# A scan and a mixture of adapters on one core: expert weights A loaded in whole rows, first units alone, SyncE holding transfers back

## The chip, the cores and the metric

The kernel runs on one core of one Trainium2 chip. The metric is the device time of one execution in microseconds; the time of a kernel is the median of its runs. The engines are called as in the profile: PE (TensorE), PEld (its weight loads), DVE (VectorE), ACT (ScalarE), POOL (GpSimd) and SP (SyncE, which here only issues transfers). HBM is the memory that holds inputs and outputs.

## The reference

Two steps are computed, both in float32. First a linear recurrence along the sequence, for 8 batches of 6400 steps and 128 channels:

```python
h = np.zeros((B, D), dtype=np.float32)
for t in range(S):
    h = a[:, t] * h + b[:, t]
    out[:, t] = h
```

Its result, seen as N = 51200 rows x of 128 channels, goes through a mixture of 8 experts of rank 16. For each row the two experts with the highest logits are taken, with softmax weights over the two:

```python
logits = x @ w_gate                                   # N x 8
topk = np.argpartition(-logits, K, axis=1)[:, :K]     # K = 2
...
delta[mask] += w[mask, k, None] * ((x[mask] @ A[e]) @ B[e])
return x + delta
```

A is 8 x 128 x 16 and B is 8 x 16 x 128, 64 KB each.

## The kernel before

The 51200 rows are cut into 100 units of 512 rows. A unit passes these stages (the numbers are the lines of the profile):

- SP loads a and b of two units in one 512 KB transfer each (line 345); a of unit 0, b of units 0 and 1 and a of unit 99 come alone, 256 KB each. Each of a and b has a ring of 8 slots of two units.
- PE transposes both into PSUM against an identity (492), so that channels lie on partitions and time along the row.
- ACT copies a out of PSUM (526, tile a_st).
- DVE runs the recurrence with one scan instruction, and a second where a batch ends in the unit (550). The scans form one serial chain. The result x stays in fp16, transposed, in the tile xT.
- PE multiplies x by the gate and by all of A at once, 8 + 128 = 136 columns per block of 128 rows (589; the 136 columns are cst_h), and ACT copies that to the tile zl (607).
- The gating finds the two best experts and their weights for a group of units: on DVE maxima (662, or 691 and 713), on POOL subtractions (672 to 735), on ACT two relus (656) and a sigmoid (745, tile g). Groups have three units, but the first four and the last ones are smaller; in the first two and the last two groups ("quick") DVE may take over steps of POOL.
- POOL, or DVE near the end, multiplies z by the expert weights (766, tile zw); PE transposes the product (774), DVE or ACT copies it out (782, zwT); PE adds x and the product with B in PSUM (802); ACT copies that to an output buffer (817, outt, 24 units); SP stores two units in one 512 KB transfer, the last two alone.

For most units two neighbours share one layout: 128 partitions hold 8 rows each of 1024. So the product of a unit waits for the scan of both units of its pair (`scanned`, and `x_block` for the layout). The units in `SOLO` have a layout of their own and wait for their own scan. Before the change those are the last two.

The order of all instructions on all engines is made by a planner in the program (`_Plan.schedule`). It goes through operations with assumed costs, latencies and priorities, and writes out one fixed list for each engine. `_Plan.run` then emits each list with semaphore waits on what an operation depends on. An engine works its list in order, so an instruction that waits holds back all that stand behind it. This holds for SP too: its transfers are issued in one fixed order. A load waits until PE has used the slot (`users`, eight pairs back); a store waits for its output copies and for the scan of the unit 20 further on (`HOLD`). Nothing in it waits for another transfer.

At the start POOL makes the identity (351, 358), and ACT issues the loads of the gate weights, B and A, in this order (345). A is read with `moe_A.rearrange("e d r -> d e r")`: 1024 runs of 16 floats, 64 bytes each. POOL casts all three to fp16 (430). PE runs ten matmuls on a zeroed tile (401, "heat") before the first transposes, and two more after each of the first five units (411, "fill"). These compute nothing that is used.

Of the kernel before, what the change touches and what calls it, by code (L numbers as in the profile page):

```python
# [15 lines left out]
    "zr": 48,  # L16
    "nout": 24,
    "hold": 20,
    "heads": (1, 1, 1, 1),
    "group": 3,  # L20
    "tails": (2, 2, 1, 1),
    "quick": (2, 2),
    "split": (4, 4),
    "solo": (0, 2),
    "mul": (0, 1, 0, 8),
    "tev": (1, 1, 4, 4),
    "tail": 8,
    "fills": 5,
    "caps": {'a': 3, 'b': 4, 'Z': 1, 'O': 3, 'w': 8},
    "least": {'Z': 1, 'O': 1},  # L30
    "pairs": (98, 2),
# [32 lines left out]
class _Plan:  # L64


    def __init__(self, sems, latency, weight, offset, switch, banks, caps, least):
# [7 lines left out]
        self.least = least  # L75
        self.ops = {}
# [12 lines left out]
    def schedule(self):  # L89
        ops = self.ops  # L90
        users = {n: [] for n in ops}
        left = {}
        glued = {op.next for op in ops.values() if op.next}
        for op in ops.values():
            op.deps = [ops[d] for d in dict.fromkeys(op.deps) if d in ops]
            left[op.name] = len(op.deps)
            for d in op.deps:
                users[d.name].append(op)
            op.key = self.weight * (op.unit + self.offset.get(op.kind, 0.0))
        end = {}  # L100
# [12 lines left out]
        while todo:  # L113
            best = None
            for e, c in cand.items():
                for x in c:
                    op = x[1]
                    if op.turn is not None and op.turn != turn:
                        continue
                    t = max(free[e], x[0])  # L120
                    takes = op.takes + (ops[op.next].takes if op.next else [])
                    if takes:
                        want = {}
                        for r, _ in takes:
                            want[r] = want.get(r, 0) + 1
                        kept = sum(max(0, k - held[r] - want.get(r, 0)) for r, k in self.least.items())
                        if len(takes) + kept > len(idle) or any(held[r] + k > self.caps[r] for r, k in want.items()):
                            continue
                        t = max(t, idle[len(takes) - 1][0])
                    if op.mode and mode and op.mode != mode:  # L130
                        t += self.switch
                    late = op.busy[e] - min(op.busy.values())
                    if best is None or (t + late, op.key) < best[:2]:
                        best = (t + late, op.key, e, x, t)
            _, _, e, pick, t = best
            for x in pick[1].engs:
                cand[x].remove(pick)
            run = [pick[1]] + ([ops[pick[1].next]] if pick[1].next else [])
            for op in run:
                for role in op.takes:  # L140
                    _, i, giver = idle.pop(0)
                    self.bank_of[role] = i
                    held[role[0]] += 1
                    if giver and giver.eng != e:
                        run[0].deps.append(giver)
            for op in run:
                turn += op.turn is not None
                op.eng = e
                mode = op.mode or mode
                self.order[e].append(op)  # L150
                free[e] = t + op.busy[e]
                t = free[e]
                if op.dma:
                    link = max(link, free[e] + 550.0) + op.dma[2]
                    end[op.name] = link + op.dma[3]
                else:
                    end[op.name] = free[e] + op.lat[e]
                if op.gives:
                    held[op.gives[0]] -= 1
                    idle.append((end[op.name], self.bank_of[op.gives], op))  # L160
                    idle.sort(key=lambda x: x[:2])
                todo -= 1
                for u in users[op.name]:
                    left[u.name] -= 1
                    if not left[u.name] and u.name not in glued:
                        for x in u.engs:
                            cand[x].append((max(end[d.name] for d in u.deps), u))
        self.span = max(end.values())
        for op in ops.values():
            if op.eng == "pe":  # L170
                op.deps = [d for d in op.deps if d.eng != "pe"]
            for d in op.deps:
# [27 lines left out]
def bass_associative_scan_2x2__then__mixture_of_adapters_kernel(  # L200
# [88 lines left out]
    with ExitStack() as stack:  # L289
# [4 lines left out]
        cst_f = sb(nc.sbuf_tensor("cst_f", [128, E + 256], F32))  # L294
        cst_h = sb(nc.sbuf_tensor("cst_h", [128, E + 256], F16))
        warm_t = sb(nc.sbuf_tensor("warm_t", [128, UT], F16))
        warm = sb(nc.sbuf_tensor("warm", [128, 1], F32))
        E_A = E + 128
        wA_h = cst_h[:, 0:E_A]
# [30 lines left out]
        dma_sem = {}  # L330

        latency = {"pe": 205.0, "dve": 170.0, "act": 230.0, "pool": 130.0, "sp": 100.0}
        plan = _Plan(sems, latency, 1000000.0, KEY, 100.0, len(psum), CFG["caps"], CFG["least"])
# [35 lines left out]

        add_dma("wg_in", "act", -110, [(cst_f[:, 0:E], moe_w_gate[:, :])], ("wg",), 80.0, (), "fix", 450.0, 2000.0)  # L370
        add_dma(
            "B_in",
            "act",
            -109,
            [(cst_f[:, E + 128 : E + 256], moe_B.rearrange("e r d -> (e r) d"))],
            ("B",),
            220.0,
            (),
            "fix",
            450.0,  # L380
            3500.0,
        )
        add_dma(
            "A_in",
            "act",
            -108,
            [(cst_f[:, E : E + 128].rearrange("d (e r) -> d e r", e=E), moe_A.rearrange("e d r -> d e r"))],
            ("A",),
            700.0,
            (),  # L390
            "fix",
            450.0,
            5500.0,
        )
        add("w0", "dve", "fix", -109, 60.0, lambda h: h.memset(warm[:, :], 0.0))
        add("table", "act", "fix", -107, 1500.0, lambda h: h.activation(warm[:, :], warm[:, :], ACTF.Sigmoid), ["w0"])
        add("wt", "dve", "fix", -109, 60.0, lambda h: h.memset(warm_t[:, :], 0.0))

        def heat(h):
            for _ in range(10):  # L400
                last = h.matmul(bank(("w", -1))[:, :], warm_t[:, 0:128], warm_t[:, :])
            return last

        add("heat", "pe", "fix", -109, 4000.0, heat, ["wt"], mode="half", takes=[("w", -1)], gives=("w", -1))

        def fill(w):


            def emit(h):
                for _ in range(2):  # L410
                    last = h.matmul(bank(("w", w))[:, :], warm_t[:, 0:128], warm_t[:, :])
                return last

            add(f"fill{w}", "pe", "fix", 1000.0, 440.0, emit, [f"AB{w}"], mode="full", takes=[("w", w)], gives=("w", w))

        for w in range(CFG["fills"]):
# [512 lines left out]
```

## Time and profile before

| | |
|---|---|
| median of 8 runs | 203.12 us (202.79 to 205.71) |
| profiled execution | 203.44 us, of which 201.4 us are the span of the profile |
| mean granted clock of TensorE | 0.992 |
| first scan starts | 6.22 us |
| first maxima of the gating (line 662) start | 12.89 us |
| last scan starts | 183.59 us |
| last output copy (line 817) ends | 198.04 us |
| HBM read, written | 52.56 MB, 26.21 MB; 391 GB/s over the span |
| load or store of 512 KB, issue to landing, median | 15.5 and 15.4 us |
| loads of gate weights, B, A, issue to landing | 3.0, 3.5 and 5.9 us |

All times of a view are counted from the start of the span. The share of an engine is its busy time over the span; instructions that only issue transfers or wait are not counted. Two rows of digits cut the span into 40 slices of some 5 us, and give a share in tenths: the clock that TensorE was granted, and the busy share of the 16 DMA engines (it can come out a little over 1, since packets overlap). The queue q1 is that of SP, q10 that of ACT; q8 brings instructions. The chain of waits is the work that ended last, followed back from the end; an entry there is a start, a duration and what it was. A line in the list of waits is the engine that waited, its line, whom it waited for, and then microseconds in total, times, and the longest.

### The profile page before, as it was taken

The page shows a single profiled execution, that of the slowest core. Times are in us where ns is not written, and L with a number is a line of the kernel's source. Part 1 is how long each engine was busy: PE and PEld are TensorE (multiplying, and loading weights), DVE is VectorE, ACT ScalarE, POOL GpSimd, SP SyncE. Part 2 cuts the span into 40 slices and gives each one's busy share as a digit, 9 for nine tenths or more (in the row PEclk, how much of TensorE's full clock was granted, in tenths as well). Part 3 has the DMA queues.
Part 4 walks back from the last instruction along what each step waited for, and adds up shares of the span by engine and source line. Part 5 has one row for each costly group of instructions (what it writes and reads, how often), then busy time and mean ns, then how long its engine had stood idle before and what let it go on. Part 6 is the DMA issues. An engine that isn't in the chain of part 4 may idle for free.

```text
span 201.4 us, 8187 instructions
## 1 busy us (share of the span) xinstructions
PE 183.6 (91%) x3204; PEld 162.1 (80%) x3204; DVE 171.5 (85%) x296; ACT 179.3 (89%) x461; POOL 157.3 (78%) x280
## 2 busy tenths in 40 slices
PE   7896999999998999997999899989999999999672
PEld 3575888988997988896898789879989889988561
DVE  1497799999999799998879887899799699797980
ACT  2386899999998998998999899999999899999862
POOL 2015378789999797888689799999998999769840
PEclk9997899999999999999999999999999999999999
DMA  6999999999999999999999999999999999986996
GB/s 209 366 410 405 410 405 405 405 409 404 409 414 411 413 418 409 412 413 417 407 411 417 407 412 415 416 413 412 418 410 410 417 410 410 410 340 263 365 408 237
DMA packets 23397, 79.30 MB, mean 394 GB/s; under 512 B 3648, under 2 KB 3776, under 8 KB 23360
## 3 DMA queue, kind: packets, MB, share of 16 engines
q1 hardware_dynamic: 22032, 78.65, 97.6%
q8 instruction: 25, 0.41, 0.8%
q10 hardware_dynamic: 1328, 0.14, 0.5%
q14 instruction: 12, 0.10, 0.1%
HBM read 52.56 MB, written 26.21 MB: 391 GB/s over the span
## 4 chain that ended last, share of the span: by engine, by line
PE 48%; ACT 19%; DVE 11%; issue 7%; DMA 6%; POOL 5%; SPq 2%; DVEq 0%
PE ps L492 17%; PE ps L802 15%; PE ps L589 8%; PE ps L774 7%; ACT zl L607 6%; DVE xT L550 6%; DMA b_in<-in_b_dram 6%; ACT outt L817 5%; ACT a_st L526 4%; POOL zw L766 4%; SPq L345 2%; ACT pn L656 2%; DVE zw L766 2%; DVE zwT L782 2%; ACT g L745 1%
## 5 line engine op out<-in xcount | busy, mean ns | idle before, releaser
L550 DVE TENSOR_TENSOR_SCAN xT<-a_st,xT,ps 128x512 f16<-128x512 f32 x96 | 120.2, 1252 | 14.1 <-ACT a_st L526 8.6
L766 POOL TENSOR_TENSOR zw<-zl,g 128x512 f16<-128x512 f32 x93 | 98.8, 1068 | 7.5 <-ACT g L745 7.5
L607 ACT COPY zl<-ps 128x408 f32<-128x408 f32 (+1 forms) x139 | 71.6, 543 | 0.2
L526 ACT COPY a_st<-ps 128x512 f32<-128x512 f32 x100 | 61.5, 641 | 11.2 <-PE ps L492 10.4
L492 PE MATMUL ps<-ident_f,a_in 64*128 64x64 f32 (+1 forms) x792 | 67.3, 229 | 3.9 <-DMA b_in<-in_b_dram 1.9
L492 PE MATMUL ps<-ident_f,b_in 64*128 64x64 f32 (+1 forms) x792 | 67.6, 230 | 1.9 <-issue 1.5
L492 PEld LDWEIGHTS ps<-ident_f,a_in 64*128 64x128 f32 (+1 forms) x792 | 56.5, 140 | 13.8 <-issue 4.3
L817 ACT COPY outt<-ps 128x512 f32<-128x512 f32 x99 | 60.7, 628 | 3.0 <-PE ps L802 2.4
L492 PEld LDWEIGHTS ps<-ident_f,b_in 64*128 64x128 f32 (+1 forms) x792 | 56.3, 140 | 1.4 <-issue 0.8
L589 PE MATMUL ps<-cst_h,xT 128*128 128x136 f16 x400 | 49.6, 235 | 0.5 <-DVE xT L550 0.2
L802 PE MATMUL ps<-ident_h,xT 128*128 128x128 f16 x400 | 43.1, 230 | 2.3 <-issue 1.3
L774 PE MATMUL ps<-ident_h,zw 128*128 128x128 f16 x400 | 38.7, 220 | 4.0 <-DVE zw L766 2.2
L589 PEld LDWEIGHTS ps<-cst_h,xT 128*128 128x128 f16 x400 | 35.8, 148 | 4.5 <-DVE xT L550 0.7
L802 PE MATMUL ps<-cst_h,zwT 128*128 128x128 f16 x400 | 38.9, 220 | 0.0
L782 DVE COPY zwT<-ps 128x256 f32<-128x256 f32 x89 | 35.8, 409 | 3.5 <-PE ps L774 3.3
L802 PEld LDWEIGHTS ps<-ident_h,xT 128*128 128x128 f16 x400 | 33.4, 148 | 4.7 <-DVE zwT L782 1.9
L774 PEld LDWEIGHTS ps<-ident_h,zw 128*128 128x128 f16 x400 | 25.2, 98 | 7.4 <-DVE zw L766 3.2
L802 PEld LDWEIGHTS ps<-cst_h,zwT 128*128 128x128 f16 x400 | 27.3, 100 | 0.0
L656 ACT ACTIVATE pn<-d 128x96 f32<-128x96 f32 (+2 forms) x72 | 23.1, 331 | 0.1
L735 POOL TENSOR_TENSOR um<-d,pn 128x96 f32<-128x96 f32 (+2 forms) x36 | 14.1, 393 | 7.0 <-ACT pn L656 6.5
L706 POOL TENSOR_TENSOR L<-zl,pn 128x96 f32<-128x96 f32 (+2 forms) x34 | 13.4, 394 | 4.7 <-ACT pn L656 3.7
L728 POOL TENSOR_TENSOR d<-d 128x96 f32<-128x96 f32 (+2 forms) x38 | 13.8, 365 | 1.5 <-DVE d L681 0.6
(31 smaller groups left out, 85.9 us busy)
## 6 DMA issues: line engine op xcount, KB each, us to landing
a_in<-in_a_dram SPq DMA_DIRECT2D x49, 512.0 KB, 15.5
b_in<-in_b_dram SPq DMA_DIRECT2D x49, 512.0 KB, 15.5
out_dram<-outt SPq DMA_DIRECT2D x49, 512.0 KB, 15.4
a_in<-in_a_dram SPq DMA_DIRECT2D x2, 256.0 KB, 9.1
b_in<-in_b_dram SPq DMA_DIRECT2D x2, 256.0 KB, 4.3
out_dram<-outt SPq DMA_DIRECT2D x2, 256.0 KB, 2.8
cst_f<-in_moe_B_dram ACTq DMA_DIRECT2D x1, 64.0 KB, 3.5
cst_f<-in_moe_A_dram ACTq DMA_DIRECT2D x1, 64.0 KB, 5.9
```

The source lines that it names most:

```text
L492: last = h.transpose(*args())
L526: lambda h: h.copy(a_st[w % NAS][:, :], bank(("a", w))[:, :]),
L550: last = h.tensor_tensor_scan(out=x_at(lo, hi), data0=a_st[w % NAS][:, lo:hi], data1=bank(("b", w))[:, lo:hi], initial=init, op0=ALU.mult, ...
L589: last = h.matmul(dst, x_block((b0 + j) // Q, (b0 + j) % Q), wA_h)
L607: return h.copy(zl[:, r0 : r0 + n, :], src)
L656: lambda h: h.activation(v(pn[s]), v(src[s]), ACTF.Relu, bias=bias, scale=scale),
L735: lambda h: h.tensor_tensor(out=v(um[s]), in0=v(d1[s]), in1=v(pn[s]), op=ALU.subtract),
L766: lambda h: h.tensor_tensor(out=oview, in0=zview, in1=gview, op=ALU.mult),
L774: last = h.transpose(dst[:, q * 128 : (q + 1) * 128], zw[v % NZW][:, q, :], ident_h[:, :])
L782: return copy(zwT[v % NZT][:, :].bitcast(F32), bank(("O", v))[:, 0 : UT // 2])
L802: last = h.matmul(bank(("O", v))[:, cols], (x_block(v, q), zwT[v % NZT][:, cols])[part], (ident_h[:, :], Bcat_h)[part], start=part == 0 an ...
L817: return copy(outt[:, v % NOUT, :], bank(("O", v))[:, :])
```

## The change

Five things are changed.

1. A is read as `(e h) (l r)`: partition e*16 + h gets the eight rows l = 0..7 of expert e that belong to block h, 512 bytes in one run, 128 runs in all. The load moves ahead of B's on ACT's queue. To bring this to the layout with d on partitions, DVE and POOL multiply the loaded tile with a mask (`mine`) into `spread`, which holds for each l a 128 x 128 matrix with a partition's values in the columns of its own expert, in fp16; and eight matmuls with 0/1 matrices (`pick`, shifted by one column for each l) add up in one PSUM bank. ACT copies the result to the fp16 tile. `mine`, `high` and `pick` are made on DVE from the identity. POOL's cast of A is gone.
2. Units 0 and 1 join the units that stand alone (`solo`): their products wait for their own scan only, and their store writes rows of 2 KB.
3. The matmuls ahead of the first transposes go from ten to six.
4. Those after the first units go from two after each of five units to two, one and one after the first three.
5. After the planner has fixed all orders, each transfer on SP's list, loads and stores alike, gets a wait for the landing of the transfer four places before it.

The planner's orders come out different on all engines after the first few instructions, since it sees the new operations; the kinds and numbers of the instructions after the start are the same, except for a few steps of the quick groups that go from POOL to DVE and one output copy that goes from DVE to ACT.

```diff
+    "flight": 4,
-    "solo": (0, 2),
+    "solo": (2, 2),
-    "fills": 5,
+    "heat": 6,
+    "filler": (2, 1, 1),
...
         self.span = max(end.values())
+        moves = [op for op in self.order["sp"] if op.dma]
+        for old, new in zip(moves, moves[self.flight :]):
+            new.deps.append(old)
...
+        pick = sb(nc.sbuf_tensor("pick", [128, 8 * 129], F16))
+        high = sb(nc.sbuf_tensor("high", [128, 16], F32))
+        mine = sb(nc.sbuf_tensor("mine", [128, E], F32))
+        spread = sb(nc.sbuf_tensor("spread", [128, 8, E, R], F16))
...
+            "A_in",
+            "act",
+            -109,
+            [(cst_f[:, E : E + 128], moe_A.rearrange("e (h l) r -> (e h) (l r)", l=8))],
...
-            "A_in",
-            "act",
-            -108,
-            [(cst_f[:, E : E + 128].rearrange("d (e r) -> d e r", e=E), moe_A.rearrange("e d r -> d e r"))],
...
-            for _ in range(10):
+            for _ in range(CFG["heat"]):
...
+        add("pick0", "dve", "fix", -109, 330.0, lambda h: h.memset(pick[:, :], 0.0))
+        add("high", "dve", ...
+                out=high[:, :], in_=ident_f[:, :].rearrange("p (e h) -> p h e", e=E), axis=AX.X, op=ALU.max
+        add("pick", "dve", ...
+                pick[:, :].rearrange("p (k c) -> p k c", c=129)[:, :, 0:128:8],
+                high[:, :].unsqueeze(1).broadcast_to([128, 8, 16]),
+        add("mine", "dve", ...
+                out=mine[:, :], in_=ident_f[:, :].rearrange("p (e h) -> p e h", e=E), axis=AX.X, op=ALU.max
+        raw = cst_f[:, E : E + 128].rearrange("p (l r) -> p l r", r=R)
+        for name, eng, lo, hi, time in (("spr0", "pool", 0, 3, 900.0), ("spr1", "dve", 3, 8, 760.0)):
+                lambda h, lo=lo, hi=hi: h.tensor_tensor(
+                    out=spread[:, lo:hi, :, :],
+                    in0=raw[:, lo:hi, :].unsqueeze(2).broadcast_to([128, hi - lo, E, R]),
+                    in1=mine[:, :].unsqueeze(1).unsqueeze(3).broadcast_to([128, hi - lo, E, R]),
+                    op=ALU.mult,
+        def gather(h):
+            for k in range(8):
+                last = h.matmul(
+                    bank(("w", -2))[:, 0:128],
+                    pick[:, k * 128 : (k + 1) * 128],
+                    spread[:, k, :, :].rearrange("p e r -> p (e r)"),
+                    start=k == 0,
+                    stop=k == 7,
+                )
+        add("selA", "pe", "fix", -107, 700.0, gather, ["pick", "spr0", "spr1"], mode="full", takes=[("w", -2)])
+        add("cstA", "act", ...
+            lambda h: h.copy(cst_h[:, E : E + 128], bank(("w", -2))[:, 0:128]),
+            ["selA"],
...
-                for _ in range(2):
+                for _ in range(CFG["filler"][w]):
...
-            ("cstA", slice(E, E + 128), 400.0, "A_in"),
```

More of the change, by code (lines that the diff above doesn't have):

```diff
@@ L64, with __init__ @@
 class _Plan:
-    def __init__(self, sems, latency, weight, offset, switch, banks, caps, least):
+    def __init__(self, sems, latency, weight, offset, switch, banks, caps, least, flight):
         self.sems = sems
@@ L75, in __init__ @@
         self.least = least
+        self.flight = flight
         self.ops = {}
@@ L332, in bass_associative_scan_2x2__then__mixture_of_adapters_kernel @@
         latency = {"pe": 205.0, "dve": 170.0, "act": 230.0, "pool": 130.0, "sp": 100.0}
-        plan = _Plan(sems, latency, 1000000.0, KEY, 100.0, len(psum), CFG["caps"], CFG["least"])
+        plan = _Plan(sems, latency, 1000000.0, KEY, 100.0, len(psum), CFG["caps"], CFG["least"], CFG["flight"])
         add = plan.add
@@ L371, in bass_associative_scan_2x2__then__mixture_of_adapters_kernel @@
         add_dma(
+            "A_in",
+            "act",
+            -109,
+            [(cst_f[:, E : E + 128], moe_A.rearrange("e (h l) r -> (e h) (l r)", l=8))],
+            ("A",),
+            220.0,
+            (),
+            "fix",
+            450.0,
+            2500.0,
+        )
+        add_dma(
             "B_in",
             "act",
-            -109,
+            -108,
             [(cst_f[:, E + 128 : E + 256], moe_B.rearrange("e r d -> (e r) d"))],
@@ L380, in bass_associative_scan_2x2__then__mixture_of_adapters_kernel @@
             450.0,
-            3500.0,
-        )
-        add_dma(
-            "A_in",
-            "act",
-            -108,
-            [(cst_f[:, E : E + 128].rearrange("d (e r) -> d e r", e=E), moe_A.rearrange("e d r -> d e r"))],
[L388 to L393, printed above, removed]
+            2500.0,
         )
@@ L399, in heat @@
         def heat(h):
-            for _ in range(10):
+            for _ in range(CFG["heat"]):
                 last = h.matmul(bank(("w", -1))[:, :], warm_t[:, 0:128], warm_t[:, :])
             return last
-        add("heat", "pe", "fix", -109, 4000.0, heat, ["wt"], mode="half", takes=[("w", -1)], gives=("w", -1))
+        add("heat", "pe", "fix", -109, 430.0 * CFG["heat"], heat, ["wt"], mode="half", takes=[("w", -1)], gives=("w", -1))
+        add("pick0", "dve", "fix", -109, 330.0, lambda h: h.memset(pick[:, :], 0.0))
@@ new lines, in bass_associative_scan_2x2__then__mixture_of_adapters_kernel @@
+        add(
+            "high",
+            "dve",
+            "fix",
+            -108,
+            220.0,
+            lambda h: h.tensor_reduce(
+                out=high[:, :], in_=ident_f[:, :].rearrange("p (e h) -> p h e", e=E), axis=AX.X, op=ALU.max
+            ),
+            ["id"],
+        )
+        add(
+            "pick",
+            "dve",
+            "fix",
+            -108,
+            220.0,
+            lambda h: h.tensor_copy(
+                pick[:, :].rearrange("p (k c) -> p k c", c=129)[:, :, 0:128:8],
+                high[:, :].unsqueeze(1).broadcast_to([128, 8, 16]),
+            ),
+            ["pick0", "high"],
+        )
@@ new lines, in bass_associative_scan_2x2__then__mixture_of_adapters_kernel @@
+        add(
+            "mine",
+            "dve",
+            "fix",
+            -108,
+            220.0,
+            lambda h: h.tensor_reduce(
+                out=mine[:, :], in_=ident_f[:, :].rearrange("p (e h) -> p e h", e=E), axis=AX.X, op=ALU.max
+            ),
+            ["id"],
+        )
+        raw = cst_f[:, E : E + 128].rearrange("p (l r) -> p l r", r=R)
+        for name, eng, lo, hi, time in (("spr0", "pool", 0, 3, 900.0), ("spr1", "dve", 3, 8, 760.0)):
+            add(
+                name,
+                eng,
+                "fix",
+                -108,
+                time,
+                lambda h, lo=lo, hi=hi: h.tensor_tensor(
[3 more added lines that the diff above has]
+                    op=ALU.mult,
+                ),
+                ["A_in", "mine"],
+            )
@@ new lines, in gather @@
+        def gather(h):
[6 more added lines that the diff above has]
+                    stop=k == 7,
+                )
+            return last
+        add("selA", "pe", "fix", -107, 700.0, gather, ["pick", "spr0", "spr1"], mode="full", takes=[("w", -2)])
+        add(
+            "cstA",
+            "act",
+            "fix",
+            -107,
+            160.0,
+            lambda h: h.copy(cst_h[:, E : E + 128], bank(("w", -2))[:, 0:128]),
+            ["selA"],
+            gives=("w", -2),
+        )
@@ L406, in fill @@
         def fill(w):
             def emit(h):
-                for _ in range(2):
+                for _ in range(CFG["filler"][w]):
                     last = h.matmul(bank(("w", w))[:, :], warm_t[:, 0:128], warm_t[:, :])
                 return last
-            add(f"fill{w}", "pe", "fix", 1000.0, 440.0, emit, [f"AB{w}"], mode="full", takes=[("w", w)], gives=("w", w))
-        for w in range(CFG["fills"]):
+            add(f"fill{w}", "pe", "fix", 1000.0, (430.0 if w == 0 else 220.0) * CFG["filler"][w], emit, [f"AB{w}"], mode="full", takes=[("w", w)], gives=("w", w))
@@ L417, in bass_associative_scan_2x2__then__mixture_of_adapters_kernel @@
+        for w in range(len(CFG["filler"])):
             fill(w)
```

## The prediction

> **What bounds the kernel now.** I read the page from the top: shares, slices, queues. The engines and the transfers are all close to full.
>
> ```profile
> PE 183.6 (91%) x3204; PEld 162.1 (80%) x3204; DVE 171.5 (85%) x296; ACT 179.3 (89%) x461; POOL 157.3 (78%) x280
> ...
> PEclk9997899999999999999999999999999999999999
> DMA  6999999999999999999999999999999999986996
> ...
> q1 hardware_dynamic: 22032, 78.65, 97.6%
> q8 instruction: 25, 0.41, 0.8%
> q10 hardware_dynamic: 1328, 0.14, 0.5%
> ```
>
> See two things: the DMA row is full until slice 35, and PEclk has a dip in slices 3 and 4. Next the windows, for the start and for the long middle (columns: PE, PEld, DVE, ACT, POOL busy, PEclk, DMA share, GB/s).
>
> ```profile
> 4.25:7.66 3.41, 3.00 (x24) 2.04 (x23) 1.22 (x1) 1.10 (x2) 0.30 (x2) 1.00 1.08 340
> 7.66:11.07 3.41, 3.08 (x43) 1.95 (x43) 2.07 (x2) 0.84 (x3) 0.27 (x1) 1.00 1.02 408
> 11.07:14.49 3.42, 3.42 (x59) 2.71 (x58) 3.29 (x9) 3.12 (x9) 0.70 (x3) 1.00 1.04 413
> 14.49:17.90 3.41, 1.84 (x34) 1.40 (x30) 3.41 (x12) 2.83 (x10) 1.94 (x5) 1.00 1.02 401
> 17.90:21.31 3.41, 3.23 (x40) 2.92 (x42) 2.26 (x4) 1.82 (x5) 1.54 (x4) 0.51 1.03 411
> ```
>
> Before 18 us ACT is idle more than it works from 4 to 11 us; the kernel lives on loads that arrive at some 410 GB/s. The chain of waits in order of time and the waits of the first 30 us say who was missing:
>
> ```profile
> 5.77 12.27 DMA b_in<-in_b_dram
> 18.08 1.12 PE ps L492 x16
> ```
>
> ```profile
> DVE xT L550 <- ACT a_st L526: 7.6, 4, 4.5
> POOL d L672 <- DVE mx L662: 5.4, 1, 5.4
> PEld ps L492 <- DMA b_in<-in_b_dram: 3.1, 3, 1.8
> ```
>
> Up to 18.08 us the chain is the load of b for units 8 and 9. After that it is engines only, to the last output copy (197.46 + 0.58 = 198.04), its 256 KB store (2.8 us) and the end of the span at 201.4. From 30 to 170 us ACT is busy 134.97 of 140 (20.00 + 47.18 + 48.65 + 19.14): in the middle it is ACT that counts.
>
> There is a second rope of nearly the same length. The trace has 16 landing marks for each transfer, one per DMA engine. The first mark of a load runs ahead of the last by 0.7 us at 15 us, 2.2 at 18, 3.8 at 78 and 6.5 at 176. So one DMA engine lags, and the last marks follow each other at 1.27 us (512 KB loads) to 1.36 us (the 16 steps from 176.64 to 198.34) without a hole from 15 us to 198.34. That engine never rests. It falls behind at instruction fetches: between the landings at 15.21 and 18.04 it lost 2.83 - 1.28 = 1.55 us beside the q8 packet at 15.9 us. Everything else waits with it, unseen by the engines' waits, since loads lead their use: the last load lands at 176.64 and its transposes run at 182.5.
>
> **The change part by part.** Sums are made against the profiled execution: 203.44 us, with a span of 201.4 and 2.04 around it. It lies 0.32 above the median of 203.12.
>
> *A in 512 B rows.* 1024 packets of 64 B (mean 11.1 ns in the trace's packet records) are 64 per DMA engine, 0.71 us. They become 128 packets like B's (27 ns), 8 per engine, 0.22 us. Every DMA engine is 0.49 us earlier from then on: b for units 8 and 9 lands at about 17.55, and the second rope ends at 198.34 - 0.49 = 197.85.
>
> *Building A.* A is now second on ACT's queue, where B was, so it lands near 4.7 us (B: 1.18 + 3.5) instead of 7.6. Added on DVE before scan 0: a memset of 516 words (256 took 0.27, so 0.54), two reductions (0.17 to 0.23 each by L691), a copy (0.23 by L418), all done by 2.9 us, in DVE's idle 4.49 us before scan 0. Then the spread of 640 elements, which waits for A. L766 on DVE took 0.67 to 1.08 us for 512 elements, more when POOL ran L766 too; so 0.84 to 1.35, ending at 5.6 to 6.1. POOL's 384 elements: 1.07 x 0.75 = 0.80. Scan 0 is queued behind the spread. It started at 6.22, because ten warm-up matmuls held transposes whose data had landed at 3.56 and 4.51. With six of them (0.43 each while slow: done at 1.22 + 2.6 = 3.8), copy and b transposes are done by 5.3, and scan 0 starts at 5.6 to 6.1: 0.1 to 0.6 sooner. The spread takes the place of the removed wait. The eight matmuls (8 x 0.06, spacing of L774) and one ACT copy of 128 elements (under the 0.36 us of 128x256; I take 0.25) end at about 7.4, before the first product can run.
>
> *First units alone.* Unit 0's products no longer wait for scan 1, nor for A at 7.64; PE gives them after b of unit 1, at about 7.8 instead of 10.78, and its maxima run at about 9.3 instead of 12.89. What follows on ACT for one unit beside the a copy is two zl (0.73 together), pn 0.23, g 0.25, zwT 0.41, outt 0.58: 2.2 us. ACT is idle 2.31 + 2.57 us between 4.25 and 11.07, and 0.58 between 14.49 and 17.90. Starting 3 us sooner moves about one unit's 2.2 us, less the new copy's 0.25, in front of 18 us. With the 0.49 that gives the engines' rope 0.5 (nothing moved; the order of the queues does not allow it) to 0.49 + 1.95 = 2.4 us. Below 0.5 only if a clock window is lost, see the rivals. I take 1.5, the middle. Store 0 becomes 2 KB rows: 256 packets of 84 ns, 1.34 us per engine against 1.28, +0.06.
>
> *The hold.* From the fifth transfer on SP waits for the fourth one before it, behind which stand all later loads and stores. PE waits for the loads and ACT for a free output buffer (24 units). Today SP already stands still: issues take 1.08 us at the median where the first took 0.43, with 15.5 us to landing, so about 12 transfers are queued. The hold moves that queue from the rings to SP, in the same order; a transfer lands when the slow DMA engine comes to it, either way. It must only find three others before it: 3 to 4 x 1.27 us, a cycle of 5.1. An unqueued 512 KB store (issued at 197.39) landed in 2.83 us, so 2.25 are to spare, and the lead that a fetch can give the other engines is 1.55. At the start, transfer 5 is issued at 3.6 instead of 2.58 while the first four keep the engines busy until about 6. I take zero. Gain bound: q8's 25 fetches took 26.8 us in sum, 1.07 each, where four 4 KB data packets take 0.64; were the excess due to the deep queue, the slow engine's four would give 4 x 0.43 = 1.7 us. Loss bound: the second rival.
>
> A rule that speaks against the hold: the Trainium skill, "DMA: Bandwidth & Descriptors", section "Latency and other measured facts", puts the access latency of HBM at 0.2 us on average and 2 us at high load. As an estimate by that page 2.83 could become 4.6; 0.5 would be left against 1.55, and up to 25 x 1.05 = 26 us could be lost. No row here shows a loaded latency without a queue.
>
> *Fewer fillers* (ten to four after the first units, ten to six before). The row 14.49:17.90 shows PE busy 1.84 us of 3.41, and the next window ran at 0.51 of the clock. So 54% busy is too little and 88% (the row 4.25:7.66) is enough. Removed are 6 x 0.22 us; A's eight matmuls and the earlier products come in. I take the dip as it is. A dip costs about 1.7 us on PE where PE is the chain (3.4 us at half speed).
>
> The Trainium skill, "TensorE: Matmul & The Clock Gate", section "What's actually happening", asks for an idle window of some 3.4 us before the clock falls. The trace disagrees: its window was 54% busy. By the page no dip threatens and the one at 18 us should not be there; by the row each starved window counts 1.7 us.
>
> **Sum.** Engines' rope: 198.04 - 1.5 = 196.5. Second rope: 197.85, plus the two single stores behind it at 0.68 each (half of 1.36): 199.2 against 200.84 now, so no more than 1.6 can be gained. Engines 1.5, less 0.06 of store 0, less some 0.1 where both ropes meet: 1.35. 203.44 - 1.35 = 202.1 for the profiled execution, 201.8 as a median.
>
> **Rivals.**
> 1. *The head start is not kept.* The orders of all queues are made anew, and ACT after 18 us has as many idle holes as before. Then 0.5 is left: 202.6. For it: ACT's 5 us of idle in 30 to 170 come from waits on PE, POOL and DVE that the change does not touch. Against: less work is left after 18 us.
> 2. *The hold dries the rings: slower.* Place: between the landing of a held transfer and the first packets of the next, on the DMA engines that no fetch has delayed. It decides from a latency under load of 2.83 + 0.7 us (2.25 to spare less 1.55). Each 0.1 us beyond costs 25 x 0.1 = 2.5 us; at 0.2 beyond 5 us, so 203.1 - 1.3 + 5 = 206.8. For it: nothing else shows a loaded latency. Against: the margin.
> 3. *One more half-speed window* at the start, with the fillers gone: +1.7, and the gain of rival 1 alone: 202.6 + 1.7 = 204.3. For it: PE has about 0.9 us of fillers less in 7.66 to 14.49. Against: both windows are over 90% busy.
> The hold doing nothing at all is part of the forecast.
>
> **How the numbers follow.** Forecast (201.8) 0.55, rival 1 0.25, rival 2 0.12, rival 3 0.08. The low end is 203.12 - 1.6 - about half of the 1.7 bound = 200.7; the high end 204.3 takes in rival 3 and leaves out rival 2. About 0.5% (1.0 us) is what a measurement of this kernel can tell from no change. Forecast: 0.8 faster, 0.2 same; rival 1: 0.2 faster, 0.8 same; rival 2 slower; rival 3: half same, half slower. Faster 0.49, same 0.35, slower 0.16.
>
> **What would show it.** A's landing near 4.7 us, scan 0 before 6.1, the first MAX8 near 9.3, b for units 8 and 9 landed by 17.6: the start is right. Transfers land about 5 us after issue, with the DMA row still full up to slice 34 and the last load landed near 176.1: the hold is free. A lower GB/s in the middle, or the last load after 177, is rival 2. A second PEclk dip is rival 3. If the start comes 3 us sooner and the last scan (183.59) does not move, rival 1. I am wrong altogether if the last scan moves by more than 2.5 us, or if landings of the middle come faster than 1.27 us apart.

## The result, and the profile after

| | |
|---|---|
| before, median of 32 runs | 203.15 us (202.53 to 205.71) |
| after, median of 11 runs | 222.94 us (218.02 to 224.1) |
| ratio after to before | 1.0822, 95% interval 1.0776 to 1.0867 |
| predicted | 201.8 us, 200.7 to 204.3 |
| profiled execution after | 226.07 us, of which 224.3 us are the span |

The change makes the kernel 8 to 10% slower. The ratio leaves out runs that lie over 1.5% above the fastest of their kernel, which leaves three of the eleven of after and is why it is below the quotient of the two medians (1.097). The profiled execution of after is 1.4% above the median, so its differences come out a little large. The page of the kernel after, from the shares of the engines to the issues of transfers:

```profile
PE 184.7 (82%) x3202; PEld 163.4 (73%) x3202; DVE 176.3 (79%) x302; ACT 182.5 (81%) x463; POOL 159.0 (71%) x278
...
PEclk9999999999999979999999999999969999999996
DMA  6998999999979998999999899999999999999996
GB/s 222 412 396 338 391 411 394 387 331 386 351 281 309 324 375 306 343 380 357 293 394 325 338 370 367 332 357 327 343 327 393 393 315 366 364 389 403 408 406 243
...
q1 hardware_dynamic: 22160, 78.65, 94.3%
q8 instruction: 26, 0.43, 0.8%
...
a_in<-in_a_dram SPq DMA_DIRECT2D x49, 512.0 KB, 5.8
b_in<-in_b_dram SPq DMA_DIRECT2D x49, 512.0 KB, 5.9
out_dram<-outt SPq DMA_DIRECT2D x49, 512.0 KB, 5.6
```

All engines work as long as before (ACT 182.5 us, was 179.3), over a span that is 23 us longer: nobody has more to do, everybody waits. The dips of PEclk are in slices 14 and 29 (counted from 0, as in the prediction), no longer in 3 and 4. Look below the DMA row, which still reads 9 nearly everywhere: the bytes tell what the busy share hides. Some 410 GB/s have become 281 to 394 from slice 8 to slice 34. And a transfer lands 5.6 to 5.9 us after its issue, where it took 15.4.

Two windows of the start and two of the middle (columns as before: PE, PEld, DVE, ACT, POOL busy, PEclk, DMA share, GB/s):

```profile
14.49:17.90 3.41, 2.28 (x48) 1.94 (x46) 3.35 (x5) 2.50 (x8) 1.72 (x4) 1.00 1.02 405
17.90:21.31 3.41, 3.36 (x62) 2.94 (x64) 3.30 (x5) 3.37 (x11) 1.40 (x6) 1.00 0.84 327
50.00:100.00 50.00, 41.83 (x771) 38.28 (x770) 41.77 (x67) 41.12 (x102) 38.11 (x64) 0.97 0.94 339
100.00:150.00 50.00, 41.58 (x751) 37.34 (x748) 37.90 (x65) 43.22 (x110) 39.93 (x68) 1.00 0.97 347
```

Up to 17.90 us nothing is wrong: 405 GB/s, and after it the clock stays at 1.00 where it was 0.51. The loss begins in the window from 17.90 (327 GB/s) and is spread over the whole middle, where ACT works 43.22 of 50 us (48.65 before). The chain of waits in order of time (start, duration, what):

```profile
2.11 5.03 DMA b_in<-in_b_dram
7.16 5.08 DMA a_in<-in_a_dram
12.26 6.17 DMA a_in<-in_a_dram
18.45 5.29 DMA a_in<-in_a_dram
...
66.56 6.80 DMA a_in<-in_a_dram
73.42 6.23 DMA a_in<-in_a_dram
```

Before, this chain left the transfers at 18.08 us and went through engines only. Now 58% of the span in it are transfers, often one behind the other: in the lines shown, each that follows another is issued 0.02 to 0.06 us after the landing that it was held for. The list of waits says the same from the engines' side:

```profile
ACT a_st L610 <- PE ps L576: 23.2, 31, 2.9
...
PEld ps L576 <- DMA a_in<-in_a_dram: 16.7, 25, 2.9
PEld ps L576 <- DMA b_in<-in_b_dram: 13.7, 18, 1.9
```

PE's weight loads wait 16.7 + 13.7 = 30.4 us for a and b at the transposes (line 576), and ACT's copy waits another 23.2 for these. Without the hold (e1, below) the three are 3.9, 2.5 and 7.1 us:

```profile
ACT a_st L610 <- PE ps L576: 7.1, 9, 2.9
...
PEld ps L576 <- DMA a_in<-in_a_dram: 3.9, 7, 2.0
...
PEld ps L576 <- DMA b_in<-in_b_dram: 2.5, 7, 0.9
```

### The profile page after: what moved, and what is told of

It is laid out like the page before. It is cut to its first block, busy times and chain, and to the rows that moved or that the text cites. A ratio compares the mean times of both kernels' runs of the same rounds, so it can differ in the third digit from the quotient of the medians.

```text
span 224.3 us, 8276 instructions
## 1 busy us (share of the span) xinstructions
PE 184.7 (82%) x3202; PEld 163.4 (73%) x3202; DVE 176.3 (79%) x302; ACT 182.5 (81%) x463; POOL 159.0 (71%) x278
## 4 chain that ended last, share of the span: by engine, by line
DMA 58%; PE 31%; DVE 3%; issue 2%; ACT 2%; POOLq 1%; POOL 1%; SPq 1%; DVEq 0%
DMA a_in<-in_a_dram 35%; DMA b_in<-in_b_dram 20%; PE ps L576 11%; PE ps L886 10%; PE ps L673 5%; PE ps L858 4%; DMA out_dram<-outt 3%; ACT outt L901 1%; DVE zw L850 1%; POOLq L295 1%; DVE xT L634 1%; SPq L355 1%; DVE zwT L866 0%; POOL d L804 0%; ACT a_st L610 0%
## 5 line engine op out<-in xcount | busy, mean ns | idle before, releaser
L576 PE MATMUL ps<-ident_f,a_in 64*128 64x64 f32 (+1 forms) x792 | 70.3, 230 | 24.2 <-DMA a_in<-in_a_dram 12.2
L576 PEld LDWEIGHTS ps<-ident_f,a_in 64*128 64x128 f32 (+1 forms) x792 | 57.5, 140 | 36.0 <-DMA a_in<-in_a_dram 16.7
L610 ACT COPY a_st<-ps 128x512 f32<-128x512 f32 x100 | 60.5, 613 | 24.3 <-PE ps L576 23.2
L691 ACT COPY zl<-ps 128x408 f32<-128x408 f32 (+1 forms) x139 | 70.5, 513 | 1.1 <-PE ps L673 1.0
L576 PE MATMUL ps<-ident_f,b_in 64*128 64x64 f32 (+1 forms) x792 | 70.2, 231 | 0.0
L901 ACT COPY outt<-ps 128x512 f32<-128x512 f32 x100 | 60.0, 610 | 5.3 <-PE ps L886 4.2
L576 PEld LDWEIGHTS ps<-ident_f,b_in 64*128 64x128 f32 (+1 forms) x792 | 57.3, 140 | 0.2
L858 PE MATMUL ps<-ident_h,zw 128*128 128x128 f16 x400 | 39.6, 223 | 3.3 <-DVE zw L850 1.9
L886 PE MATMUL ps<-cst_h,zwT 128*128 128x128 f16 x400 | 39.8, 223 | 1.4 <-issue 1.4
L740 ACT ACTIVATE pn<-d 128x96 f32<-128x96 f32 (+2 forms) x72 | 21.5, 307 | 0.7 <-POOL d L782 0.6
```

Source lines behind the costliest of these rows:

```text
L576: last = h.transpose(*args())
L610: lambda h: h.copy(a_st[w % NAS][:, :], bank(("a", w))[:, :]),
L691: return h.copy(zl[:, r0 : r0 + n, :], src)
L740: lambda h: h.activation(v(pn[s]), v(src[s]), ACTF.Relu, bias=bias, scale=scale),
L858: last = h.transpose(dst[:, q * 128 : (q + 1) * 128], zw[v % NZW][:, q, :], ident_h[:, :])
L886: last = h.matmul(bank(("O", v))[:, cols], (x_block(v, q), zwT[v % NZT][:, cols])[part], (ident_h[:, :], Bcat_h)[part], start=part == 0 an ...
```

## The experiments

Most readings below are of landing marks. **Step** is the mean distance between the last marks of transfers that land one after the other; **first mark** is the time from issue to the first of a transfer's 16 marks, **spread** the time from there to the last. All are worked out from the trace, for the transfers whose last mark lies in the stretches 10 to 50, 50 to 100 and 100 to 150 us:

| kernel | in flight | time, us | step, us | first mark + spread, 50 to 100 us |
|---|---|---|---|---|
| before | no hold | 203.15 | 1.33, 1.30, 1.29 | 12.83 + 2.95 |
| after | 4 | 222.94 | 1.38, 1.58, 1.54 | 3.65 + 2.59 |
| e1, after without the hold | no hold | 202.57 | 1.31, 1.29, 1.29 | 11.76 + 3.73 |
| e2, before with the hold | 4 | 221.06 | 1.32, 1.43, 1.48 | 3.52 + 2.13 |
| e3 | 8 | 203.58 | 1.30, 1.27, 1.31 | 6.79 + 3.28 |
| e4 | 6 | 203.4 | 1.33, 1.28, 1.28 | 3.92 + 3.58 |
| e6 | 5 | 203.62 | 1.34, 1.28, 1.32 | 4.14 + 2.23 |
| e7, loads alone held | 4, and stores | 208.48 | 1.47, 1.31, 1.31 | 4.91 + 2.41 |
| d1, transfers alone | 16 | 194.77 | 1.28, 1.25, 1.25 | 13.79 + 1.53 |
| d2, transfers alone | 4 | 204.41 | 1.28, 1.31, 1.38 | 3.76 + 1.48 |
| d3, with matmuls | 4 | 218.95 | 1.39, 1.48, 1.42 | 3.73 + 2.15 |
| d4, with matmuls | 16 | 198.9 | 1.33, 1.29, 1.26 | 12.51 + 3.10 |
| d5, with matmuls | 5 | 199.53 | 1.32, 1.29, 1.28 | 3.82 + 2.58 |

d1 to d5 are single executions; the other times are medians, and the landing marks are those of one profiled execution each.

### The hold taken out, and the hold alone

e1 is the kernel after with a limit that is never reached; e2 is the kernel before with the hold and nothing else.

```diff
-    "flight": 4,
+    "flight": 1000,
```

> The changed kernel with the wait on the fourth transfer before taken out; all else is as changed. Theory D (the hold lets the DMA engines run dry: a held transfer needs 3.7 to 4.8 us from its issue to the first landing mark where I took 2.8, so a fetch of instructions that delays one DMA engine delays all): 201.8 us, 0.990 to 0.997 of before, the middle at 410 GB/s and 512 KB landing 15 us after issue. Theory S (the new start, or the orders that the planner made anew, cost the time): 218 us or more. Theory P (the waits themselves are what costs SP, whatever they wait for): 202 as D.

```diff
         self.span = max(end.values())
+        moves = [op for op in self.order["sp"] if op.dma]
+        for old, new in zip(moves, moves[4:]):
+            new.deps.append(old)
```

> The kernel before with the wait on the fourth transfer before added and nothing else. D: some 223 to 226 us (the 21.1 us that the change lost against the forecast of 201.8, on top of 203.1), 340 to 350 GB/s in the middle, landing 5 to 6 us after issue. S: 203 us. P: as D.

e1: 202.57 us (201.94 to 203.66, 12 runs), ratio to before 0.997 (0.9947 to 0.9993). e2: 221.06 us (218.8 to 225.96, 4 runs), ratio 1.0826 (1.0765 to 1.0887). The hold alone brings the whole loss, and the rest of the change a small gain. That speaks against theory S. e2 lies below the 223 to 226 us that theory D expected, and its middle moves 366 GB/s where 340 to 350 were expected: D has the place and the sign, and its size is somewhat too large. The page of e1:

```profile
PEclk9999999999999999999999999999999999999998
DMA  6999999999999999999999999999999999996995
GB/s 204 366 420 408 408 408 406 405 411 405 407 422 413 415 419 413 411 416 419 411 415 414 415 413 414 418 415 416 415 419 414 414 413 419 412 370 257 404 402 221
...
a_in<-in_a_dram SPq DMA_DIRECT2D x49, 512.0 KB, 15.4
```

405 to 422 GB/s from slice 2 to slice 34, and 15.4 us to landing, as before the change. Between 10 and 175 us the steps of after are longer than those of e1 by 2.1, 8.9, 8.2 and 3.1 us in sum (the fourth stretch is 150 to 175 us): 22.3 of the 23.4 us between the two profiled executions. So the loss is in the steps and nowhere else.

### How many must be in flight

Three kernels change the limit alone.

```diff
-    "flight": 4,
+    "flight": 8,
```

> The changed kernel with the wait moved to the eighth transfer before. Eight transfers are 10.2 us of work for each DMA engine, against a landing of 3.7 to 4.8 us and a lead of some 4 us. D: the engines hardly run dry, 201.5 to 204 us, over 400 GB/s in the middle. P: the waits are as many as with four, so 215 us or more. S: 218 or more.

> The changed kernel with the wait moved to the sixth transfer before: 7.6 us of work in flight, against a landing of 3.7 to 4.8 us, so the other engines can lead the slowest by some 3 us where the trace of before has leads up to 6.5 us. D: between the ends, 203 to 210 us, and 385 to 410 GB/s in the middle. P: 215 or more. S: 218 or more.

> The changed kernel with the hold at the fifth transfer before, 6.4 us of work in flight; four gave 222.9 us and six 203.4. Theory F says that the loss is what a fetch costs beyond the lead which the window leaves, so one transfer more (1.27 us) takes away about that much from each of 25 fetches: 203 to 209 us. If it is a fixed number of round trips that counts, half of the loss stays: 211 to 215 us.

Eight, six and five give 203.58, 203.4 and 203.62 us (10 runs each), ratios 0.9994 (0.9961 to 1.0028), 0.9987 (0.996 to 1.0014) and 1.0003 (0.9966 to 1.004). All three agree with before, none with after. It is no slope but a step, between five and four. SP waits as often with five, six and eight as with four, but for a few waits at the start, so the waits themselves cost nothing that is seen here (theory P). The page of e6:

```profile
GB/s 212 369 418 407 408 362 347 409 412 404 406 418 415 411 420 410 411 410 403 416 398 410 413 414 417 410 411 386 407 384 397 387 396 393 417 411 408 413 407 120
...
a_in<-in_a_dram SPq DMA_DIRECT2D x49, 512.0 KB, 6.4
```

A transfer takes 6.4 us here, more than the 5.8 of after, and still the bytes flow. What counts is not the time of one transfer but that time over the number in flight: 6.24 us (3.65 + 2.59) shared by four is a step of 1.56, and 6.37 us (4.14 + 2.23) shared by five is 1.27, which is what the DMA engines can do (1.25 to 1.28 in d1). Where each transfer waits for the landing of the one k places before, step times k must equal this sum; so the sum alone tells no cause. The packets of the trace do. From 50 to 100 us, fewer than 16 packets were under way in 39% of the time in after, in 0.6% of it in e6, and never in before and e1: with four in flight, DMA engines ran dry. That is about half of the loss (14.96 packets at a time in the mean, 16.43 in before). The other half is that a packet of 4 KB took 0.180 us in the mean in place of 0.161, by a few packets of up to 1.94 us, while the median is 0.159 in both. Since a packet that takes long counts as busy, the share fell by less than the bytes: from 1.03 to 0.94, where 412 GB/s became 339. Whether these packets are a cause of the empty engines or come of them is open.

### The transfers by themselves

These kernels leave out the whole computation and store a constant. They move the same 100 loads and 50 stores of 512 KB; two of them let PE run 3200 matmuls beside it, which bring 25 instruction fetches (0.41 MB on q8).

```diff
             for n, (kind, t, k) in enumerate(moves):
                 if n >= HOLD:
                     h.wait_ge(*landed[n - HOLD])
...
             for _ in range(MATMULS):
                 h.matmul(ps[:, 0:128], warm_t[:, :], warm_t[:, :])
```

> Transfers alone: 100 loads and 50 stores of 512 KB issued by SP in the order of the real kernel (40 loads, then two loads and a store in turn, then 20 stores), each held back until the transfer 16 places before has landed; no engine computes, and the output holds a constant. Both theories: 150 x 1.27 to 1.31 us and about 5 around it, 194 to 202 us, over 405 GB/s.

> The same transfers alone, each held back until the one four places before has landed; no engine computes. Theory F (four in flight are enough, and it takes the instruction fetches, each of which stops one DMA engine for 1 us or more, to make the held engines run dry): within 3 us of the one with sixteen. Theory L (the latency under load alone is over what four transfers cover): 15 to 25 us longer than that, some 350 GB/s.

> As the one before, four in flight, and PE runs 3200 matmuls of 128 columns on a constant beside it, which bring about 25 fetches of 16 KB of instructions and touch nothing that is transferred. F: 15 to 25 us longer than without the matmuls. L: no change from them, within 3 us.

> Sixteen in flight and the 3200 matmuls beside it. F: each DMA engine meets its own fetches only, so at most 4 x 1.5 = 6 us longer than sixteen in flight without the matmuls, with the first and the last landing mark of a transfer drifting apart. L: the same as without the matmuls.

The rows of bytes of d2 and then of d3:

```profile
GB/s 228 358 398 417 414 408 408 411 410 408 409 417 415 389 387 418 387 374 401 396 383 389 395 380 383 379 358 379 386 375 380 387 371 376 414 417 419 412 415 277
```

```profile
GB/s 225 389 393 383 378 381 395 284 405 346 340 407 335 381 348 360 324 384 369 400 359 402 386 406 352 361 331 346 335 302 381 371 390 314 399 414 412 407 407 261
```

In d2 the loads alone (to some 54 us) run at 398 to 417 GB/s from slice 2 on: with nothing else going on, four are enough, at 5.10 us from issue to landing. When stores come between the loads it falls to 358 to 418, and with stores alone at the end it is back at 412 to 419. In the mixed part some packets of 4 KB take 1.0 to 1.9 us (0.67 was the longest of d1, which moves some 420 GB/s in its mixed part). With the matmuls (d3) the loads alone suffer too. In time: going from sixteen to four costs 204.41 - 194.77 = 9.6 us without matmuls and 218.95 - 198.9 = 20.1 us with them; the matmuls cost 4.1 us with sixteen in flight and 14.5 us with four. Each is a difference of two single executions; the runs of before lie 3.2 us apart, so the 4.1 is little more than what runs differ by.

The 9.6 us lie between what theory F (within 3) and theory L (15 to 25) expected of d2, and the 14.5 just below F's 15 to 25 for d3. So neither theory stands alone: there is a loss without any fetch, which comes with loads and stores side by side, and a larger one with the matmuls and their fetches. Both show as delays of some DMA engines against the others (the spread is 1.48 us in d2 and 2.15 in d3), which four transfers do not bridge.

### Where the fillers stand

```diff
-    "flight": 4,
+    "flight": 1000,
-    "filler": (2, 1, 1),
+    "filler": (2, 2, 2, 2, 2),
```

> The changed kernel without the hold, and with two filler matmuls after each of the first five units again. Theory C (what the change without the hold gains, 0.6 us at the median where 1.35 was forecast, is cut by half-speed windows at the start, which fall in some executions because PE has less to do): 201.6 to 202.2 us, ratio to before 0.992 to 0.996, no half-speed window before 25 us. Theory R (the second rope, the slowest DMA engine, ends it at the same time whatever the start does): 202.4 to 202.9 us as without the fillers.

203.13 us (202.38 to 204.51, 12 runs), ratio 0.9997 (0.9968 to 1.0026), against 0.997 of e1. Putting the fillers back after the first units gains nothing. The time lies above what both theories expected; no window before 25 us runs at half speed, as theory C asked, and yet the gain did not come, so C is not the reason.

### Loads alone held, and five without the computation

In e7 stores wait for no transfer, so that one or two stores come on top of four loads; d5 is d3 with a limit of five.

```diff
-        moves = [op for op in self.order["sp"] if op.dma]
+        moves = [op for op in self.order["sp"] if op.dma and op.name.startswith("ld")]
```

> The kernel after, but only loads wait for the fourth load before them; stores wait for no transfer. So four loads are in flight as before, and up to two stores beside them. Theory N (what counts is how many transfers are queued, whatever their kind; with five or six the delays of single DMA engines no longer reach the end): from the first stores on there are five in flight part of the time, so most of the loss is gone: 203 to 208 us, with the first 50 us like those of the changed kernel (mean step of the last marks 1.38 us) and the steps of 50 to 150 us near 1.30 to 1.40. Theory M (stores in flight hold up the loads, so four loads beside stores are as slow as before): 215 to 223 us, steps of 50 to 150 us at 1.5 us.

> The kernel that only moves data (100 loads and 50 stores of 512 KB, 3200 matmuls with their instruction fetches, nothing computed that is used, a constant stored) with five transfers in flight in place of four (218.95 us) or sixteen (198.9). Theory N: five suffice here as in the full kernel (222.9 with four, 203.6 with five): 199 to 203 us, steps of the last marks near 1.30 us in all phases. Rival: five suffice in the full kernel only since its other waits hide the loss; then the transfers alone lie between, at 206 to 214 us, with holes over 1.6 us left in 50 to 150 us.

e7: 208.48 us (207.31 to 209.92, 4 runs; before beside it 203.7), ratio 1.026 (1.0193 to 1.0327). d5: 199.53 us. The row of bytes of e7:

```profile
GB/s 224 410 391 384 313 317 338 395 390 394 391 419 404 414 418 413 415 412 419 412 396 414 410 408 413 415 388 409 403 390 403 357 404 394 391 415 415 418 415 101
```

One kernel shows both regimes. Until slice 9 (some 51 us) only loads are under way, four of them, and the row falls to 313. From the first stores on (53 us) a fifth and sixth transfer are in flight, and up to the last slice it is at 388 to 419, but for one slice at 357. The step of 10 to 50 us is 1.47, worse than the 1.38 of after, though up to the first store both kernels wait alike: so much can two executions differ. Afterwards it is 1.31, as expected of theory N; the time is just above N's 208 and far from the 215 that M asked for. d5 is within 0.6 us of sixteen in flight (198.9) and 19.4 below four: the step between four and five is a matter of the transfers, not of the kernel's other waits.

## Why the prediction was wrong, point by point

**The start: right.** A landed at 4.61 us (4.7 predicted), DVE's spread took 0.83 (0.84 to 1.35), scan 0 began at 5.71 (5.6 to 6.1), the first MAX8 at 9.48 (9.3), b of units 8 and 9 landed at 17.14 (17.55). POOL's share of the spread was mis-sized, 1.47 us for 0.80, but it ended at 6.16 and held up nothing: PE stood at the transposes of a load that landed at 6.49, and the eight matmuls ran behind them, from 7.18. So the copy of A ended at 8.11 in place of 7.4, in time for the first zl at 8.57.

**The head start and the second rope: right in the profile, too large in the median.** e1 is this part by itself. Its last output copy ends at 195.69 us (196.5 predicted, 198.04 before), its last landing is at 199.42 (199.2 predicted, 200.84 before), and the stores' last marks are still 1.24 to 1.39 us apart from 179.40 to 198.16. That the second rope caps the gain, as the prediction said, fits these marks. But the medians differ by 0.55 us, not 1.35; the interval allows 0.14 to 1.08. The profiled execution of e1 gains 1.5 us of span, of which 0.7 are lost again around it (2.73 us, 2.04 before). Where that comes from stays open.

**The fillers: right that nothing is lost by them.** In e1 the window 14.49:17.90 has PE busy for 2.57 us, where it was 1.84, and the next one runs at full clock: the earlier products do what the fillers did. e5 shows no gain from more of them. Rival 3's extra window is seen in the profiles of e3 (6.8 us at half speed) and e4 (3.4 us), whose medians are those of before.

**The hold: the step that failed.** The prediction wrote "It must only find three others before it: 3 to 4 x 1.27 us, a cycle of 5.1. An unqueued 512 KB store (issued at 197.39) landed in 2.83 us, so 2.25 are to spare, and the lead that a fetch can give the other engines is 1.55" and then "I take zero". Three things in this sentence were wrong.
- *The latency.* 2.83 us was taken from the quiet end of the run. In the middle of after the first mark alone comes 3.65 us after the issue, up to 4.8 (issued at 86.94, first mark at 91.70). The deep queue of before hid this, since there a transfer has been waiting for 12 us when its turn comes.
- *The lead.* 1.55 us is what one fetch gave at the start. The mean spread in after is 2.59 us between 50 and 100 us. The prediction had itself read 2.2 to 6.5 us of spread in before, and then set only the first jump against the margin. Under the hold of four it rests there, presumably since faster DMA engines cannot get further ahead than the transfers that are in flight; with sixteen and matmuls it goes on growing (3.10 us in 50 to 100, 4.33 in 100 to 150 in d4).
- *The sum.* 3.65 + 2.59 = 6.24 us is over 5.1 by 1.1. That is a mean over all transfers of 50 to 100 us (5.46 in 10 to 50 us, 6.01 in 100 to 150), where the prediction looked for an excess once for each fetch.

One reading beside these was slightly off, and nothing rests on it: SP's issues before took 1.05 us at the median, not 1.08.

An example from after: b issued at 55.07 us has its first mark only at 58.81, 2.37 us after that of the transfer before it, and a fetch of 1.50 us falls on 59.22. The last marks jump from 58.78 to 62.77 us, and the next transfer that waits for this one is issued at 62.86, 4.0 us after the one before it. With a deep queue a slow DMA engine delays only itself and the others work on, as the growing spread shows; here it delays all sixteen. This fits the 4.1 us of the matmuls becoming 14.5.

**Rival 2 named the mechanism and was mis-sized.** Place and sign are those of the runs; of the causes it had the fetches, but not the loss that comes without any (9.6 us in d2): "a lower GB/s in the middle, or the last load after 177" came out as 339 to 347 GB/s and a last load at 200.55. Its price, 25 fetches of 0.2 us beyond the margin, gave 206.8; the measured loss of the hold is 222.94 - 202.57 = 20.4 us between the medians (17 us by the ratios, 1.0822 less 0.997). The threshold of 3.53 us was passed already by the mean first mark. The chance of 0.12 rested on the margin of 2.25 us, which had one row behind it, taken where nothing else moved.

The prediction weighed the page "DMA: Bandwidth & Descriptors" of the Trainium skill, section "Latency and other measured facts", against this row: an access latency of 2 us at high load, from which it made a loss of up to 26 us. The runs are on the page's side, with 20.4 us, though they don't show what part of the 3.65 us is the memory's. That 26 came so near is partly luck, since it counted the fetches alone.

The page "Runtime: NRT & Kernel Launch" of the Trainium skill, section "Instruction fetch mechanics", calls the cost of crossing an instruction block mostly hidden. What it costs the engine that fetches, no run here shows. The transfers are another matter: 3200 matmuls with 25 fetches cost 4.1 us in d4 against d1, and 14.5 us in d3 against d2. What part of it is the fetches' own was not tried apart from the matmuls.

## What to carry to other kernels

A limit on transfers in flight is priced by (issue to first landing under load + spread between the DMA engines) over the number in flight, against the step that the DMA engines can do; with 512 KB transfers this was 6.2 us against 1.28, so that five were enough and four cost 20 us. Take both from the loaded middle of a run with a short queue: before shows 12.83 + 2.95 us, most of it time in the queue, and its quiet end 2.83 us, and neither foretells the 6.2. Without such a run keep a deeper queue, which cost nothing here. Only transfers of 512 KB on one queue were tried, so whether it is their number or their bytes that counts is open. A DMA row of nines proves nothing about throughput; read the bytes below it and the distance of the landings.

## What was not expected of the hardware

- *Mixed directions.* Four transfers of 512 KB in flight keep 16 DMA engines full with loads alone (5.10 us each, no hole to 54 us in d2) and with stores alone, but not when both alternate: single 4 KB packets then take up to 1.9 us, and the rate falls from some 410 to some 380 GB/s. With sixteen in flight (d1) the same order runs at some 420 GB/s, and no 4 KB packet from 10 to 150 us takes over 0.33 us.
- *Fetches take part in the jam.* The q8 packets took 0.88 to 2.53 us in after (1.17 in the mean), and 0.96 to 1.34 in before (1.07).
- *The clock.* Windows of 3.41 us at full clock in which PE was busy for up to 1.62 us (47%, in e7) were followed by one at half speed, among them 0.71 (e2), 1.06 and 1.58 (after) and 1.59 (e3). Those with 1.94 us (57%, late in before) or more were not, as 2.07 (e5), 2.28 (after) and 2.57 (e1). Between them both happened: half speed after 1.84 us in before and in e4, full speed after 1.78 us late in e4 and at the end of the matmuls in d4. So the prediction's reading of busy shares holds, but its 54% lies in a range where the share alone does not decide. Two lines of after show a case:

```profile
77.34:80.75 3.41, 1.06 (x22) 0.99 (x23) 1.28 (x1) 0.55 (x2) 0.81 (x3) 1.00 0.93 340
80.75:84.16 3.41, 3.41 (x35) 3.21 (x35) 1.86 (x3) 2.24 (x7) 2.69 (x4) 0.50 1.02 370
```

So a stall of the loads can cost twice, since PE, starved for 2.35 of 3.41 us, gets its clock back only a window later. There are two such places in after (80.75 and 162.67 us), some 3.4 us of PE's time in all by the prediction's 1.7 each.
